# Split output products for the second half of the first span, and a float32 attention product for the second span

## The chip, the cores and the metric

The kernel runs on one core of one Trainium2 chip. The metric is the device time of one execution in microseconds (us), lower is better. The core has a matrix engine (PE) that multiplies a stationary 128x128 operand with a moving one and accumulates in PSUM banks, a vector engine (DVE), a scalar engine (ACT), GpSimd (POOL) and SyncE (SP). In this kernel POOL and SP hardly do more than issue transfers: each has its own queue, and both queues are served by the same 16 DMA engines.

## The reference

Per head: a softmax over the features of q, a softmax over the sequence of k, a 64x64 product k^T v, and q times that product. The heads are joined to rows of 512, and a gated layer follows. All is float32.

```
q_s = exp(q - max(q, axis=-1));  q_s = q_s / (sum(q_s, axis=-1) + 1e-9)
k_s = exp(k - max(k, axis=2));   k_s = k_s / (sum(k_s, axis=2) + 1e-9)
kv  = einsum('bhsd,bhse->bhde', k_s, v)
x   = einsum('bhsd,bhde->bhse', q_s, kv)   # -> (4608, 512)
out = (1 / (1 + exp(-(x @ w_gate))) * (x @ w_val)) @ w_out
```

There are 8 batches of 576 tokens and 8 heads; w_gate and w_val are 512x1536, w_out is 1536x512. The three weights arrive as float64 words.

## The kernel before

The 4608 tokens are worked in nine spans of 512. The first span (span 0) is special: while it runs, the weights are read, narrowed from float64 to float32, split into a high and a low fp32r part, and saved to DRAM for the later spans. It has twelve steps, j = 0 to 11, one for each 128 columns of w_gate and w_val. A step has a first product (`g1_0`, L690: eight float32 matmuls of 512 columns), a sigmoid and a gate product (`g_sig_0` on ACT, `g_mul_0` on DVE, L702), and, one step late, the output product of the step before (`g2_0(j-1)`, L724: four float32 matmuls of 512 columns into the four accumulators). The later spans use three fp32r products of the split parts instead (high x high, high x low, low x high): `g1` (L742, in seven smaller products over sums of blocks) and `g2` (L814), in six steps each.

Beside the first span's matmuls, DVE and ACT narrow the next weights (`w_low`, `w_top`, `w_join`, `wo_...`; L165, L171, L182, L186), cast the parts (`wo_hi` on ACT L244 and `wo_save` on DVE L248, then a POOL transfer; `split_hi` on ACT L293 and `split_lo` on DVE L298, then POOL transfers L303), and prepare the second span: its k, v and q rows (L392, L397, L345), its k^T v (`k_mm`, L420, PE), and its attention product (`x_mm`, L606), which takes three fp32r products per head pair from the parts of q (`qT_hi` on ACT, `qT_lo` on DVE L574) and of k^T v (`kv_hi`, `kv_lo`).

The order on each engine is the order in which the code is written; nothing is reordered. Buffers come from pools, and a semaphore wait stands wherever a buffer is still in use. SP's transfers go through eight semaphores in turn (DMAHW0 to DMAHW7): a transfer waits until the one eight places earlier has landed.

Two places matter further on. One is the end of the first span: step 11 leaves DVE with `split_lo`, the differences `c_lo` (L670) for the next span, `g_mul_0(11)` and the last two `wo_save`. The span's last output product, `g2_0(11)`, stands on PE behind the second span's first `g1`. The other is the third step of the second span: there PE does `k_mm(2)`, which needs rows 0 to 575 of v of batch 2. Rows 0 to 255 lie in two buffers, v_0 and v_1; before, `load_next(1, 5, range(2))` in step 10 asks SP for them, behind the k rows of batch 2.

## Time and profile before

| | us |
|---|---|
| median of 3 runs | 927.94 (927.7 to 928.8) |
| the profiled execution, its own time | 928.79 |
| its span in the profile | 927.0 |
| PE busy | 915.6 (99% of the span) |
| DVE busy | 610.7 (66%) |
| ACT busy | 474.7 (51%) |
| POOL busy | 170.0 (18%) |

The profile gives, for each engine, when its instructions ran and what ended each idle time. "Idle before" with an engine or a DMA behind an arrow says who was waited for. The first span runs from 0 to about 172 us, the second starts its first products at 157 us. Ends of matmuls are modelled, so a group's cost is read from the start of one group to the start of the next.

### The profile page before, as it was taken

How to read it: one execution, taken by the hardware profiler on the slowest of the kernel's cores; microseconds unless marked ns; L12 is line 12 of the kernel's file. 1: busy time of each engine (PE TensorE's matmuls, PEld its weight loads, DVE VectorE, ACT ScalarE, POOL GpSimd, SP SyncE). 2: the span in 40 equal slices, each digit the busy share in tenths (PEclk: the TensorE clock that was granted, in tenths of full speed). 3: DMA queues.
4: the chain of work that ended last, by engine and by line, in shares of the span. 5: the costliest groups of instructions: out<-in, count | busy, mean ns of one | idle time of the engine just before them, and what ended most of it. 6: DMA issues, size and time to landing. Idle time of an engine off the chain costs nothing.

```text
span 927.0 us, 18677 instructions
## 1 busy us (share of the span) xinstructions
PE 915.6 (99%) x7598; PEld 839.6 (91%) x7598; DVE 610.7 (66%) x987; ACT 474.7 (51%) x798; POOL 170.0 (18%) x321
## 2 busy tenths in 40 slices
PE   7999999999999999999999999999999999999998
PEld 7445545899999999999999999999999999999998
DVE  8899979756767577666766667666846574664242
ACT  2777886545445445644563456354725443543222
POOL 0010101312121212212221222112122122212220
PEclk9999999999999999999999999999999999999999
DMA  9987676999999989998999999999997799768761
GB/s 312 371 302 294 256 256 241 396 354 312 260 294 338 321 254 248 337 310 298 240 315 326 292 250 299 317 291 256 303 295 214 226 261 322 235 186 257 213 208 69
DMA packets 93556, 257.97 MB, mean 278 GB/s; under 512 B 15192, under 2 KB 17760, under 8 KB 90528
## 3 DMA queue, kind: packets, MB, share of 16 engines
q0 software_dynamic: 44576, 168.32, 59.8%
q1 hardware_dynamic: 48896, 88.47, 32.2%
q8 instruction: 60, 0.98, 0.5%
q14 instruction: 24, 0.20, 0.1%
HBM read 228.20 MB, written 28.56 MB: 277 GB/s over the span
## 4 chain that ended last, share of the span: by engine, by line
PE 81%; issue 8%; DMA 5%; DVE 4%; POOL 1%; SPq 1%; ACT 0%; POOLq 0%; DVEq 0%
PE gv L742 48%; PE acc L814 28%; DMA wo_raw<-wo_in 2%; PE gv L606 2%; PE at L420 2%; DMA ring<-qf_in 1%; DMA s_sb<-s 1%; DMA lent<-k_in 1%; PE at L606 1%; SPq L385 1%; POOL s L303 1%; DVE f_w L186 0%; POOL wo L251 0%; DVE wo_hl L248 0%; DVE h L702 0%
## 5 line engine op out<-in xcount | busy, mean ns | idle before, releaser
L742 PE MATMUL gv<-c_hl,s_sb 128*128 128x256 f32 x2304 | 277.3, 276 | 0.8 <-DMA s_sb<-s 0.8
L814 PE MATMUL acc<-wo_hl,h 128*128 128x256 f32 x2304 | 269.6, 276 | 0.0
L742 PEld LDWEIGHTS gv<-c_hl,s_sb 128*128 128x128 f32 x2304 | 268.7, 188 | 0.9 <-DVE q_m L498 0.9
L814 PEld LDWEIGHTS acc<-wo_hl,h 128*128 128x128 f32 x2304 | 264.8, 188 | 0.4
L742 PE MATMUL gv<-c_hl,a_w 128*128 128x256 f32 x1728 | 220.8, 277 | 1.9 <-DVE h L702 1.9
L742 PEld LDWEIGHTS gv<-c_hl,a_w 128*128 128x128 f32 x1728 | 207.2, 188 | 3.0 <-DVE h L702 2.1
L310 POOL DMA_DIRECT2D s_sb<-s x188 | 101.4, 539 | 301.5 <-PE gv L742 301.4
L768 DVE TENSOR_TENSOR sg<-gv,sg 128x512 f32<-128x512 f32 x48 | 33.2, 692 | 153.5 <-PE gv L742 153.5
L260 POOL DMA_DIRECT2D wo_hl<-wo x96 | 51.7, 539 | 283.1 <-PE acc L814 280.5
L760 ACT COPY sg<-gv 128x512 f32<-128x512 f32 x48 | 28.2, 588 | 131.8 <-PE gv L742 131.3
L770 ACT COPY sg<-gv 128x512 f32<-128x512 f32 x48 | 28.2, 587 | 104.8 <-PE gv L742 104.8
L772 DVE TENSOR_TENSOR sg<-sg 128x512 f32<-128x512 f32 x48 | 33.2, 692 | 57.3 <-ACT sg L770 57.3
L690 PE MATMUL gv<-x,f_w 128*128 128x512 f32 x160 | 70.2, 593 | 0.0
L690 PEld LDWEIGHTS gv<-x,f_w 128*128 128x128 f32 x160 | 30.0, 190 | 36.3 <-issue 34.5
L793 DVE TENSOR_TENSOR h<-sg,h 128x1024 fp32r<-128x1024 f32 x48 | 58.8, 1226 | 1.6
L781 DVE TENSOR_TENSOR sg<-sg 128x512 f32<-128x512 f32 x48 | 33.2, 693 | 33.6 <-ACT sg L775 33.6
L775 ACT ACTIVATE sg<-sg 128x512 f32<-128x512 f32 x48 | 30.5, 634 | 46.2 <-DVE sg L774 46.2
L762 ACT COPY sg<-gv 128x512 f32<-128x512 f32 x48 | 28.2, 587 | 37.7 <-PE gv L742 37.7
L765 ACT COPY sg<-gv 128x512 f32<-128x512 f32 x48 | 28.2, 587 | 37.2 <-PE gv L742 37.2
L724 PE MATMUL acc<-wo_t,h 128*128 128x512 f32 x96 | 43.2, 592 | 0.0
L724 PEld LDWEIGHTS acc<-wo_t,h 128*128 128x128 f32 x96 | 18.2, 190 | 22.5 <-issue 22.2
L774 DVE TENSOR_TENSOR sg<-gv,sg 128x512 f32<-128x512 f32 x48 | 33.2, 692 | 2.4
(160 smaller groups left out, 999.2 us busy)
## 6 DMA issues: line engine op xcount, KB each, us to landing
s_sb<-s POOLq DMA_DIRECT2D x188, 512.0 KB, 7.3
wo_hl<-wo POOLq DMA_DIRECT2D x96, 512.0 KB, 5.9
s<-s_sb POOLq DMA_DIRECT2D x12, 1024.0 KB, 5.9
out<-x SPq DMA_DIRECT2D x35, 256.0 KB, 5.4
ring<-k_in SPq DMA_DIRECT2D x28, 256.0 KB, 6.0
ring<-qn_in SPq DMA_DIRECT2D x28, 256.0 KB, 4.9
four<-q_m_row SPq DMA_DIRECT2D x56, 128.0 KB, 11.8
ring<-qT_in SPq DMA_DIRECT2D x28, 256.0 KB, 10.3
```

The costliest lines, as they stand in the source:

```text
L260: nc.gpsimd.dma_start(out=t.rearrange("p h e -> p (h e)"), in_=wo_dram[2 * p + i].bitcast(F32R))
L310: nc.gpsimd.dma_start(out=s_sb[:, i].rearrange("p h n e -> p (h n e)"), in_=s_dram[p][:, i * n:(i + 1) * n].bitcast(F32R),)
L690: nc.tensor.matmul(ps[n], lhsT=w[:, kt // 2, sl], rhs=x_0[:, kt], start=(kt == 0), stop=(kt == NK - 1),)
L724: nc.tensor.matmul(acc[0][m], lhsT=h_0[j][:, m * P:(m + 1) * P], rhs=wo_t[j // 2][:, j % 2], start=(j == 0), stop=(j == NJ - 1),)
L742: nc.tensor.matmul(ps[:, n], lhsT=lh(kt), rhs=c_hl[i][:, x, kt], start=(first and n == 0 and kt == 0 and lh is wh and x == 0), stop=(last ...
L768: nc.vector.tensor_tensor(out=sg[:, 0], in0=rr, in1=sg[:, 0], op=ALU.add)
L772: nc.vector.tensor_tensor(out=sg[:, 3], in0=sg[:, 3], in1=sg[:, 2], op=ALU.add)
L774: nc.vector.tensor_tensor(out=sg[:, 1], in0=z, in1=sg[:, 1], op=ALU.add)
L775: nc.scalar.activation(sg[:, 0:2, 0], sg[:, 0:2, 0], AF.Sigmoid)
L781: tt(out=sg[:, 0:2, 0], in0=sg[:, 0:2, 0], in1=sg[:, 0:2, 1], op=ALU.mult)
L793: nc.vector.tensor_tensor(out=lo, in0=sg[:, :, 0], in1=hi.bitcast(F32), op=ALU.subtract)
L814: nc.tensor.matmul(acc[w][m][:, es], lhsT=h[lh][:, i, sl], rhs=o[i][:, rh, es], start=(at == 0 and i == 0 and lh == 0 and rh == 0 and e == 0),
```

## The change

- `g2_0(j)` for j from 6 on is done in three fp32r products with 256 columns each, six matmuls for each accumulator in place of one of 512 float32 columns. The parts of w_out are the ones that `wo_hi` and `wo_save` make for DRAM anyway; they are now kept for the product. The parts of h are new: a cast on ACT (`h_hi_0`) and a subtraction on DVE (`h_lo_0`). `wo_hi(j-1)` and `h_hi_0(j-1)` move to the head of step j on ACT, `wo_save(j-1)` and `h_lo_0(j-1)` stand in front of `w_low` on DVE.
- In step 11 `g_mul_0(11)` moves ahead of the splits on DVE, and so do `wo_save(10)` and `h_lo_0(10)`.
- For steps 10 and 11, h lies in the buffers v_0 and v_1 (v_two). The rows of v of batch 2 that belong there are no longer loaded in step 10, but by `after_second`, behind everything that the second span's first step asks SP for.
- The second span's attention product takes q and k^T v in float32 (`x_mm_1`: two float32 matmuls, of 64 and 448 columns, per head pair). `kv_copy_0` and `kv_copy_1` write the block matrices to v_0 and v_1, `q_copy_1` copies q out of PSUM. `qT_lo`, `qT_hi` and `kv_split(0)` go.
- At the start, operations on neighbouring blocks of q and k are joined (two maxima of 1024 instead of four of 512, and so on), and the last two k blocks get one subtraction and one exponential.
- Of the narrowing, the sign bits of weight tiles 6 and 7 move from DVE to ACT; where DVE still does it, it is one operation on whole words.
- Two k loads and five v loads for the second span stand after step 0 and step 1 instead of in the opening.

On DVE, from the sums of the last split (L272, L273) to the first differences for the next span, before:

```order
L272 TENSOR_TENSOR four_111<-f_last_118 128x512 [waits DVE_49]
L272 TENSOR_TENSOR four_111<-four_111,f_last_118 128x512 [waits DVE_49]
L272 TENSOR_TENSOR four_111<-f_last_118 128x512
L272 TENSOR_TENSOR four_111<-f_last_118,four_111 128x512 [waits DVE_49]
L186 SCALAR_TENSOR_TENSOR wo_t_952<-wo_t_952,wo_raw_903 128x512 [waits Activation_49]
L298 TENSOR_TENSOR a_w_1079<-f_last_118,a_w_1079 128x2x512 [waits Activation_49]
L670 TENSOR_TENSOR c_hl_1061<-x_32_109,c_hl_1061 128x512
```

The same place on DVE now:

```order
L273 TENSOR_TENSOR four_111<-f_last_118 128x512 [waits DVE_49]
L273 TENSOR_TENSOR four_111<-four_111,f_last_118 128x512 [waits DVE_49]
L273 TENSOR_TENSOR four_111<-f_last_118 128x512
L273 TENSOR_TENSOR four_111<-f_last_118,four_111 128x512 [waits DVE_49]
L249 TENSOR_TENSOR wo_hl_1125<-wo_t_962,wo_hl_1125 128x512 [waits DMASW0_49,Activation_49]
L770 TENSOR_TENSOR h_p_1127<-v_0_113,h_p_1127 128x512 [waits Activation_49]
L187 SCALAR_TENSOR_TENSOR wo_t_962<-wo_t_962,wo_raw_896 128x512
L762 TENSOR_TENSOR v_1_114<-gv_1116,v_1_114 128x512 [waits PE_49,Activation_49]
L299 TENSOR_TENSOR a_w_1130<-f_last_118,a_w_1130 128x2x512 [waits Activation_49]
L726 TENSOR_TENSOR c_hl_1107<-x_32_109,c_hl_1107 128x512
```

`wo_save(10)`, the new `h_lo_0(10)` and `g_mul_0(11)` now stand ahead of the splits; before, `wo_save(10)` and `g_mul_0(11)` stood behind the last difference.

On SP, the end of the first span's loads and the second span's first step, before (q_m_row and q_r_row are the maxima and factors of q for the third span, `four` their copies over the partitions, `out` the first span's result, kt the transposed k of batch 3):

```order
L371 DMA ring_1057<-k_in 64x512 [waits DMAHW7_49,DVE_49,Activation_49]
L387 DMA v_0_113<-v_in 128x512 [waits DMAHW0_49]
L387 DMA v_1_114<-v_in 128x512 [waits DMAHW1_49]
L387 DMA f_last_118<-v_in 128x512 [waits DMAHW2_49,PE_49,Activation_49]
L387 DMA f_last_118<-v_in 128x512 [waits DMAHW3_49,PE_49]
L387 DMA f_last_118<-v_in 64x512 [waits DMAHW4_49,PE_49]
L490 DMA q_m_row_1232<-q_m_1227 128x32 [waits DMAHW5_49,DVE_49]
```

SP now, from the transposed k of batch 3 on:

```order
L331 DMA kt_0_115<-kT_in 128x576 [waits DMAHW0_49]
L331 DMA kt_1_116<-kT_in 128x576 [waits DMAHW1_49]
L559 DMA four_111<-q_m_row_1303 64x512 [waits DMAHW3_49,DMAHW2_49]
L559 DMA four_111<-q_m_row_1303 64x512
L559 DMA four_111<-q_m_row_1303 64x512 [waits DMAHW4_49]
L559 DMA four_111<-q_m_row_1303 64x512 [waits DMAHW5_49]
L559 DMA four_111<-q_m_row_1303 64x512 [waits DMAHW6_49]
L559 DMA four_111<-q_m_row_1303 64x512 [waits DMAHW7_49]
L559 DMA four_111<-q_m_row_1303 64x512 [waits DMAHW0_49]
L559 DMA four_111<-q_m_row_1303 64x512 [waits DMAHW1_49]
L398 DMA v_0_113<-v_in 128x512 [waits DMAHW2_49]
L398 DMA v_1_114<-v_in 128x512 [waits DMAHW3_49]
```

The two v loads have moved behind q_m_row, four `out`, two kt and eight `four` transfers, and each of them waits for the landing of a `four` transfer eight places ahead of it (the first and the second).

The diff, cut to its core:

```diff
@@ narrowing
     def narrow_sign_bits(raw):
-        nc.vector.tensor_scalar(
-            out=half(raw, U16, 1), in0=half(raw, U16, 3), scalar1=2 ** 15, scalar2=None,
-            op0=ALU.bitwise_and,
+        low = word(raw, 0)
+        nc.vector.scalar_tensor_tensor(
+            out=low, in0=word(raw, 1), scalar=-2 ** 31, in1=low,
+            op0=ALU.bitwise_and, op1=ALU.bitwise_or,
         )
...
     def w_on_vector(j):
-        return j in (1, 6, 7)
+        return j == 1
@@ second span's attention product
+    kv_1 = [v_two[b].rearrange("p (h e) -> p h e", e=P) for b in range(2)]
...
+    def x_mm_1(hp):
+        x_ps[1, hp] = ps = ps_at.tile([P, T], F32, name="at")
+        q = q_1.pop(hp)
+        for b, f, t in x_parts(1):
+            nc.tensor.matmul(
+                ps[:, f:t], lhsT=kv_1[b][:, hp], rhs=q[:, f:t],
+                start=True, stop=True, skip_group_check=True,
+            )
@@ output product of the first span
     def g_sig_0(j):
-        h_0[j] = two.tile([P, T], F32, name="h_0", tag="h_lo")
+        if j < J3:
+            h_0[j] = two.tile([P, T], F32, name="h_0", tag="h_lo")
+        else:
+            h_0[j] = v_two[j % 2] if j > 9 else ring.tile([P, T], F32, name="ring")
...
+    def h_hi_0(j):
+        h_hl[0, j] = t = two.tile([P, 2, T], F32R, name="h_p", tag="h_lo")
+        nc.scalar.copy(out=t[:, 0], in_=h_0[j])
+
+    def h_lo_0(j):
+        t = h_hl[0, j]
+        nc.vector.tensor_tensor(
+            out=t[:, 1], in0=h_0.pop(j), in1=t[:, 0].bitcast(F32), op=ALU.subtract
+        )
...
+            h, o = h_hl[0, j], wo_out[j]
+            for lh, rh in ((0, 0), (0, 1), (1, 0)):
+                for e in range(2):
+                    es = slice(e * HT, (e + 1) * HT)
+                    nc.tensor.matmul(
+                        acc[0][m][:, es], lhsT=h[:, lh, sl], rhs=o[:, rh, es],
...
@@ loads
         if j == 10:
             k_max_rows(2)
-            load_next(1, 5, range(2))
+            load_next(1, 5, ())
...
+    def after_second():
+        for t in range(2):
+            v_load(2, t)
@@ start
     k_exp(0, 0)
-    for c in range(NC):
-        qn_sub(0, c)
-        qn_exp(0, c)
+    for c in (0, 2):
+        qn_sub(0, c, 2)
+        qn_exp(0, c, 2)
...
-    for t in ORDER_0[1:]:
+    for t in (3, 4):
         k_sub(0, t)
         k_exp(0, t)
         k_mm_0(t, kv0)
-    for c in range(NC):
-        qn_sum(0, c)
+    k_subs(0, 1, 3)
+    k_exps(0, 1, 3)
+    k_mm_0(1, kv0)
+    k_mm_0(2, kv0)
+    qn_sum(0, 0, NC)
     warm(12)
@@ steps of the first span
         beside_first(j)
+        if j > 0:
+            wo_hi(j - 1)
+        if j > J3:
+            h_hi_0(j - 1)
...
         wo_join(j)
+        if j > J3:
+            wo_save(j - 1)
+            h_lo_0(j - 1)
...
@@ step 11
     g1_0(j)
+    wo_hi(j - 1)
+    h_hi_0(j - 1)
+    g_sig_0(j)
     split_hi(p, (0, 3))
-    wo_hi(j - 1)
+    wo_save(j - 1)
+    h_lo_0(j - 1)
     wo_join(j)
-    g_sig_0(j)
+    g_mul_0(j)
     g2_0(j - 1)
@@ later spans
                 side_b(w + 1, at)
+            if (w, at) == (1, 0):
+                after_second()
```

## Rows read from the trace of the kernel before

**Rows 1.** The page's first part (busy time and share of each engine), and the waits of PE after its first matmuls, from the view of who waited for whom (total us, times, longest).

```profile
PE 915.6 (99%) x7598; PEld 839.6 (91%) x7598; DVE 610.7 (66%) x987; ACT 474.7 (51%) x798; POOL 170.0 (18%) x321
...
PE gv L742 <- DVE h L702: 1.9, 1, 1.9
```

**Rows 2.** PE in order of time: start, duration, what. Steps 9 to 11 of the first span (counted from 0), then the second span up to its fourth step.

```profile
132.52 3.60 PE L724 MATMUL acc<-wo_t,h 128*128 128x512 f32 x8
...
136.90 7.03 PE L690 MATMUL gv<-x,f_last 128*128 128x512 f32 x16
143.77 3.60 PE L724 MATMUL acc<-wo_t,h 128*128 128x512 f32 x8
147.20 0.27 PE L355 MATMUL at<-ident,k_max 128*4 128x128 f32 x1
...
169.29 3.59 PE L724 MATMUL acc<-wo_t,h 128*128 128x512 f32 x8
...
175.06 3.06 PE L742 MATMUL gv<-c_hl,s_sb 128*128 128x256 f32 x24 [0.76 <-DMA s_sb<-s]
...
199.25 1.15 PE L420 MATMUL at<-v,ring 128*64 128x64 f32 x32
...
201.87 5.72 PE L814 MATMUL acc<-wo_hl,h 128*128 128x256 f32 x48
207.43 1.52 PE L742 MATMUL gv<-c_hl,a_w 128*128 128x256 f32 x12
```

**Rows 3.** All engines in order of time, the opening: PE's k^T v product (L405), its filler matmuls (L1042), ACT's exponentials of k (L397), the transposes of q (L552).

```profile
16.85 2.35 ACT L397 ACTIVATE lent<-lent 128x512 f32<-128x512 f32 x4
17.57 2.38 PE L405 MATMUL acc<-lent 128*64 128x65 f32 x64
...
19.88 2.94 PE L1042 MATMUL gv<-lent 128*128 128x128 f32 x24
22.66 0.60 PE L552 MATMUL gv<-ident,lent 128*128 128x128 f32 x4
```

**Rows 4.** DVE in order of time, from the gate product of step 9 to the third span's first maxima.

```profile
132.72 0.69 DVE L702 TENSOR_TENSOR h<-gv,h 128x512 f32<-128x512 f32 x1 [1.61 <-PE gv L690]
...
155.38 0.69 DVE L670 TENSOR_TENSOR c_hl<-x,c_hl 128x512 fp32r<-128x512 f32 x1
156.50 1.23 DVE L298 TENSOR_TENSOR s_sb<-four,s_sb 128x1024 fp32r<-128x1024 f32 x1 [0.43 <-ACT s_sb L293]
...
163.59 1.28 DVE L248 TENSOR_TENSOR wo_hl<-wo_t,wo_hl 128x512 fp32r<-128x512 f32 x2
...
172.79 2.46 DVE L498 TENSOR_REDUCE q_m<-ring 128x8 f32<-128x512 f32 x4
```

**Rows 5.** SP's issues in order of time (start, time until the last of the group was issued, what).

```profile
159.52 2.88 SPq L387 DMA_DIRECT2D v<-v_in  x2
...
175.28 0.34 SPq L490 DMA_DIRECT2D q_m_row<-q_m  x1
175.71 1.81 SPq L717 DMA_DIRECT2D out<-x  x4
177.56 0.99 SPq L329 DMA_DIRECT2D kt<-kT_in  x2
181.85 12.98 SPq L530 DMA_DIRECT2D four<-q_m_row  x8
195.74 0.33 SPq L490 DMA_DIRECT2D q_r_row<-q_r  x1
197.31 1.66 SPq L537 DMA_DIRECT2D ring<-qT_in  x2
```

**Rows 6.** DMA issues of short stretches (KB of each, median us from issue to landing): the v rows at 159.4 to 161.3 us, the first `four` at 178 to 182, those at 182 to 184, and the first q^T row at 197 to 198.5; then DVE's work on those q^T rows by the view of the tile `four`.

```profile
v<-v_in SPq DMA_DIRECT2D x1, 256.0 KB, 6.5
...
four<-q_m_row SPq DMA_DIRECT2D x1, 128.0 KB, 13.8
...
four<-q_m_row SPq DMA_DIRECT2D x3, 128.0 KB, 14.9
...
ring<-qT_in SPq DMA_DIRECT2D x1, 256.0 KB, 11.2
...
L541 DVE TENSOR_TENSOR ring<-ring,four x4: 684/692/694, 208.6 to 211.6; 128x512 f32<-128x512 f32 x4
```

**Rows 7.** Stretches: busy time of PE, PEld, DVE, ACT and POOL (instructions), granted PE clock, DMA share, GB/s. The last two are of the very start.

```profile
195.00:200.00 5.00, 5.00 (x62) 4.87 (x62) 2.74 (x5) 3.08 (x5) 1.08 (x2) 1.00 1.32 300
200.00:205.00 5.00, 5.00 (x89) 4.87 (x86) 2.62 (x5) 0.00 (x0) 0.00 (x0) 1.00 1.37 340
...
3.00:4.00 1.00, 1.00 (x6) 1.00 (x6) 0.96 (x2) 0.00 (x0) 0.00 (x0) 1.00 1.04 340
...
10.00:11.00 1.00, 1.00 (x12) 1.00 (x11) 1.00 (x2) 0.00 (x0) 0.00 (x0) 1.00 1.03 383
```

**Rows 8.** PE at the very start, in order of time: the filler matmuls, the transposes of k behind the first pause, the next fillers.

```profile
1.14 5.84 PE L1042 MATMUL gv<-lent 128*128 128x128 f32 x32 [1.14 <-POOL lent L1005]
9.38 0.63 PE L1056 MATMUL acc<-ident,lent 128*128 128x128 f32 x4 [2.40 <-DVE lent L1053]
9.85 1.50 PE L1042 MATMUL gv<-lent 128*128 128x128 f32 x12
```

**Rows 9.** POOL in order of time: the first load of the sums' weights (s_sb) for the second span's second step; it stands right behind the save of the last w_out tile.

```profile
165.91 0.54 POOL L310 DMA_DIRECT2D s_sb<-s  x1
```

More of the change, by code (lines that the diff above doesn't have):

```diff
@@ L36 @@
 ORDER_0 = (0, 3, 4, 1, 2)
+J3 = 6
 NF = 2
@@ L340, in k_max, with k_max_1 @@
             out=kneg[b][:, hp:hp + 1], in0=m, scalar1=-1.0, scalar2=None, op0=ALU.mult
+        )
+    def k_max_1():
+        kmax[1], kneg[1], ksum[1] = (
+            small.tile([P, NP], F32, name=f"k_{x}") for x in ("max", "neg", "sum")
+        )
+        nc.vector.tensor_reduce(out=kmax[1].unsqueeze(2), in_=k1T, axis=AX.X, op=ALU.max)
+        nc.vector.tensor_scalar(
+            out=kneg[1], in0=kmax[1], scalar1=-1.0, scalar2=None, op0=ALU.mult
         )
@@ L392, in k_sub, with k_subs @@
         eng.tensor_tensor(out=kt[:n], in0=kt[:n], in1=kmb[b][:n], op=ALU.subtract)
+    def k_subs(b, t0, t1):
+        kt = k_rows[b][:, t0:t1]
+        m = kmb[b].unsqueeze(1).broadcast_to([P, t1 - t0, DM])
+        nc.vector.tensor_tensor(out=kt, in0=kt, in1=m, op=ALU.subtract)
     def k_exp(b, t):
@@ L475, in attn_moe, with qn_of @@
     qn_sb = {}
+    q_rows = {}
+    def qn_of(w, c, n):
+        if n == 1:
+            return qn_sb[w, c]
+        return q_rows[w][:, c:c + n].rearrange("p c (i d) -> p (c i) d", d=D)
     q_m = {}
@@ L515, in qn_sum @@
         nc.vector.tensor_reduce(
-            out=q_r[w][:, c * TI:(c + 1) * TI], in_=t, axis=AX.X, op=ALU.add
+            out=q_r[w][:, c * TI:(c + n) * TI], in_=t, axis=AX.X, op=ALU.add
         )
-        if c == NC - 1:
+        if c + n == NC:
             t = q_r[w]
@@ L610, in x_mm, with kv_copy_0, kv_copy_1, q_copy_1 @@
                     )
+    q_1 = {}
+    kv_1 = [v_two[b].rearrange("p (h e) -> p h e", e=P) for b in range(2)]
+    def kv_copy_0():
+        for b in range(2):
+            nc.scalar.copy(out=kv_1[b], in_=kv_0)
+    def kv_copy_1():
+        for a in range(2):
+            sl = slice(a * D, (a + 1) * D)
+            nc.scalar.copy(out=kv_1[1][sl, :, sl], in_=kv_32[1](sl))
+    def q_copy_1(hp):
+        q_1[hp] = t = ring.tile([P, T], F32, name="ring")
+        nc.scalar.copy(out=t, in_=qT_sb.pop((1, hp)))
+    def x_mm_1(hp):
[5 more added lines that the diff above has]
+                start=True, stop=True, skip_group_check=True,
+            )
     def x_ev(w, hp):
@@ L723, in g2_0 @@
         for m in range(NT):
-            nc.tensor.matmul(
-                acc[0][m], lhsT=h_0[j][:, m * P:(m + 1) * P], rhs=wo_t[j // 2][:, j % 2],
-                start=(j == 0), stop=(j == NJ - 1),
-            )
+            sl = slice(m * P, (m + 1) * P)
+            if j < J3:
+                nc.tensor.matmul(
+                    acc[0][m], lhsT=h_0[j][:, sl], rhs=wo_t[j // 2][:, j % 2],
+                    start=(j == 0), stop=False, skip_group_check=True,
+                )
+                continue
+            h, o = h_hl[0, j], wo_out[j]
+            for lh, rh in ((0, 0), (0, 1), (1, 0)):
+                for e in range(2):
+                    es = slice(e * HT, (e + 1) * HT)
+                    nc.tensor.matmul(
+                        acc[0][m][:, es], lhsT=h[:, lh, sl], rhs=o[:, rh, es],
+                        start=False, stop=(j == NJ - 1 and lh == 1 and e == 1),
+                        skip_group_check=True,
+                    )
         if j == NJ - 1:
@@ L941, in behind_joins @@
             kv_lo(1)
-        if 6 <= j <= 9:
-            qT_lo(1, j - 6)
     def after_first(j):
         if j == 0:
-            for hp in range(NP):
-                k_max(1, hp)
+            k_max_1()
+            for t in range(3, 5):
+                k_load(1, t)
         if j == 1:
@@ L952, in after_first @@
                 qn_max(1, c)
+            for t in range(5):
+                v_load(1, t, v1[t])
         if j == 2:
@@ L1031, in attn_moe @@
         qn_load(1, c)
-    for t in range(5):
+    for t in range(3):
         k_load(1, t)
-    for t in range(5):
-        v_load(1, t, v1[t])
+    q_rows[0] = q0
+    k_rows[0] = k0
     idle = ps_gv.tile([P, T], F32, name="gv")
@@ L1087, in attn_moe @@
         k_mm_0(t, kv0)
-    for c in range(NC):
-        qn_sum(0, c)
+    k_subs(0, 1, 3)
[3 more added lines that the diff above has]
+    qn_sum(0, 0, NC)
     warm(12)
-    for hp in range(NP):
-        qf_mul(0, hp)
-        if hp == 0:
-            k_done_0(kv0)
+    qf_mul(0, 0)
+    k_done_0(kv0)
+    qf_mul(0, 1, NC - 1)
     w_low(0)
@@ L1194, in attn_moe @@
     wo_hi(j)
-    g_mul_0(j)
-    wo_save(j - 1)
+    h_hi_0(j)
     wo_save(j)
+    h_lo_0(j)
     def wo_next(w, at):
```

61 lines of the change are left out of this document (32 added, 29 removed).

## The prediction

> **What bounds the kernel now.** I read the page's first part, the waits of PE, PE in order of time, then the same stretch on DVE, on SP's queue and by landings. PE is busy 99% of the span [rows 1]. From its first weight product on, each group starts where the one before ends, but for two waits: 1.9 us for a DVE result at the end of the first span [rows 1] and 0.76 us for a weight load [rows 2]. So each us saved on PE counts, as long as nothing that PE waits for is late. The reader is to see two things that already run close. DVE works through the first span's end without a pause but for 0.43 us [rows 4]. And from about 160 us on both DMA queues are full: in the third step of the second span they move 300 to 340 GB/s with a DMA share of 1.3 [rows 7], and what SP asks for takes 11 to 15 us to land [rows 6].
>
> **The opening.** PE does the last two k blocks from 19.2 us on and starts 12 fillers (24 instructions) at 19.88; the transposes of q follow at 22.66 without a pause, so the opening ends on PE [rows 3]. Now the last two exponentials are one, behind a subtraction that is one too; I reckon its end at about 19.3 instead of 16.85 + 2.35 = 19.2. Only then PE starts two blocks, not one. Four blocks took 2.31 us (17.57 to 19.88), 0.58 each, so the fillers start at about 20.5, and all behind them is 0.6 us later. The bounds are 0, if the joined operations on DVE bring the exponential forward by as much, and 0.8. What they save shortens a chain that doesn't end here, so I take +0.6.
>
> **The output products.** Float32 costs 143.77 to 147.20, 3.43 us a step. Three fp32r products in the later spans take 201.87 to 207.43, 5.56 for 48, so 2.78 for 24 [rows 2]. Six steps save 0.65 each, 3.9 us. The bound below is 0: if the kept parts come late, PE waits instead.
>
> **The attention product.** Step 9 takes 4.38 us from its output product to the next first product; less 3.43 this leaves 0.95 for six fp32r matmuls [rows 2]. Float32 with 448 columns is 448/512 of 0.858, 0.75; the 64 columns cost between 0.11 (in proportion) and 0.23, a filler of 128 columns (24 instructions in 2.78, two to a matmul [rows 3]). So 0.86 to 0.98: I take no change, four times. DVE loses `qT_lo`, four times 0.6 us, and ACT gets `kv_copy` in its place; both lie beside step 6's first product of 6.9 us.
>
> **The casts.** `h_lo_0` costs DVE 0.6 us each (two of this form in 1.28 [rows 4]). PE waits for it at the fifth of six matmuls, about 0.45 us into the group. At the end that bites: from the gate product of step 9, which waits for PE, DVE has 32.15 us of work until `wo_save(11)` is through (132.72 to 164.87 [rows 4]); now 1.2 more, less the pause of 0.43. With the opening's +0.6 and two cheaper products, PE ends step 9's first product at 132.0 instead of 132.52; so DVE ends at 165.0 instead of 164.87. PE gets no faster than that: `c_lo(B11)`, at 155.38 before [rows 4], now has `wo_save(10)`, `h_lo_0(9)`, `h_lo_0(10)` and `g_mul_0(11)` ahead of it, starts at 157.2, and the second span's first products follow DVE. They end about 167.7 instead of 169.29. The wait of 1.9 us is gone, since the gate product that it was for is early; waits for the casts, by the same reckoning some 0.3, 1.1 and 1.2 us in steps 8, 10 and 11, take its place. `g2_0(11)` is 0.65 cheaper: the second step starts 2.2 us earlier. Its load of s_sb is issued at 165.7 as before (165.91, landed 174.92 [rows 2, 9]), since it stands behind `wo_save(11)`; between 6.5 and 9 us of landing PE is 2.6 to 0.3 us ahead there. Half a MB of v and half a MB of w_out no longer stand right before it, some 2.5 us at 400 GB/s, so I take the upper end. **If nothing else moved**, PE would reach `k_mm(2)` at 196.6 instead of 199.25, and the time would be 927.94 - 2.6 = 925.3.
>
> **The v rows.** Here the change pays. `k_mm(2)` begins with v_0 and v_1. Before, they were asked for at 159.52 [rows 5] and had 40 us. Now they stand behind q_m_row, `out`, kt and eight `four`, and each waits for the landing of one of the first two `four`. Before, those were issued from 181.85 on and landed after 13.8 and 14.9 us, at 195.65 and 197.2; the two transfers that stood in that place, q_r_row and the first q^T row, were issued at 195.74 and 197.31 to the landing [rows 5, 6]. What sets this chain is `q_m_row`, which follows DVE's maxima after the second span's first step; I have that 1.5 us earlier. So v_0 goes out at about 194, v_1 at 195.5. PE wants them at 196.6 and 197.1. Bounds of the landing: a 256 KB row of v took 6.5 us at 160 us [rows 6], which gives v_1 at 201.5 to 202. The first q^T row took 11.2, landed at 208.5, and DVE started on it at 208.6 [rows 6]: the same size, the same place behind the `four`. With 1.5 us less and one more row that is v_1 at 207.7. I take 205.7, near the upper end, since POOL's queue, which shares the engines, has its last requests 2.6 us earlier and half a MB less. PE's first matmul on v_1 was at 199.25 + 0.49. The time moves by 205.7 - 199.7 = **+6.0 us**, between +1.8 and +8.0, whatever PE won before: all gains ahead of this wait become wait. Behind PE's wait stand `g2` of the second span and all that follows, in the order of the code; the q^T rows, which now land behind v, are due 6 us later too.
>
> Of the queues: SP's transfers got about 87 GB/s while POOL's were queued (128 KB every 1.5 us). The Trainium skill's page "DMA: Bandwidth & Descriptors", section "Queues, rings and completion order", says that each DMA engine goes round in turn between the queues that have work; the trace agrees, and by it SP speeds up once POOL's queue is empty.
>
> **The clock.** PE would stand idle some 9 us. The trace has one pause to compare: 2.40 us, after which 12 fillers' instructions come at full pace [rows 8]. The other end is the start, after doing nothing: 6 matmuls in a us where later 12 fit, 32 in 5.84 us [rows 7, 8] where 24 took 2.78 [rows 3], so 2.1 us lost, though the clock column says 1.00 throughout [rows 7]. 6 a us against 12 are the two levels, 1.2 and 2.4 GHz. Bounds 0 and 2.1; I take 2.1, since nine us of nothing are nearer to a start than to 2.4 us.
>
> The Trainium skill's page "TensorE: Matmul & The Clock Gate", Part 1, says that an idle engine falls back to half its clock and must work to regain it. By it the whole 2.1 us is due; by the one pause of the trace alone, none.
>
> **The sum.** Profiled execution: 928.79 + 6.0 + 2.1 = 936.9, its span 927.0 + 8.1 = 935.1. It lies 0.85 above the median, so from 927.94: **936.0**.
>
> **The rivals.** (a) The wait comes, the clock holds: +6.0, 933.9. For it: the pause of 2.40 us cost nothing. (b) The v rows land at the quick end, 201.5 to 203.5: +1.8 to +3.8, about 930.7. For it: 6.5 us once; against it: eight `four` ahead in a full queue. (c) The other side: v lands before PE wants it, and the gain of 2.6 us stays, 925.3. It decides at the landing of v_1: faster if that is before 199.7 minus 1.9, that is within 2.3 us of its issue, or if SP reaches these rows much earlier than the chain q_m_row, `out`, kt, `four` lets it. The rows give no such landing. (d) In between, v_1 at 198 to 201.5: within 1.9 us of before. (e) The split products aren't cheaper than float32: PE comes to `k_mm(2)` at 199 or later and waits there just the same; the time is that of the forecast, and only PE's rows would tell.
>
> **Chances.** Forecast with the clock lost 0.50; (a) 0.17; (b) 0.15; (d) 0.10; (c) 0.08; (e) is inside the first two. A measurement of this kernel can tell about 0.2%, 1.9 us, from no change. So slower 0.82, same 0.10, faster 0.08. The range leaves out (c) and most of (d): from 929.7, the quick landing without clock loss, to 939.0, which is +8.0 and 2.1 with 0.9 on top for the opening and for what I took too early on SP.
>
> **What would show it.** Right: one wait of PE of 7 to 11 us in the second span, at the first or second group of `k_mm(2)`, ended by a v row; v_0 issued at 193 to 195 us; matmuls behind it at half the pace for a few us. Right on the small steps: first weight product at 29.4 to 29.6 instead of 28.87; output products of 2.7 to 2.8 us; no wait for the gate product at the end of the first span. Wrong, if v lands before PE comes, if the wait is below 3 us, or if PE stalls for something else, above all for the casts of steps 9 and 10 by more than 2 us.

## The result, and the profile after

The changed kernel takes **940.42 us** (median of 4 runs, 938.1 to 941.04) beside 928.37 us for the kernel before (4 runs, 927.7 to 931.07): ratio 1.0115, 95% interval 1.0096 to 1.0135. The profiled execution of the changed kernel is 940.6 us long with a span of 938.6, so 11.6 us of span more than before. All executions on record are undisturbed ones; the ratios with their intervals are estimates over them and not the quotients of the two medians beside them.

The waits of PE (us in total, times, longest), from the view of who waited for whom, changed kernel. Waits of its first 30 us are left out:

```profile
PE at L440 <- DMA v<-v_in: 6.7, 2, 5.9
PE gv L824 <- DMA s_sb<-s: 2.7, 1, 2.7
...
PE acc L805 <- DVE wo_hl L249: 1.1, 2, 0.7
...
PE gv L824 <- DVE c_hl L726: 0.3, 1, 0.3
```

The wait for the gate product at the end of the first span [rows 1] is gone. Four others are there, and the first is the one forecast: PE waits for the rows of v. PE in order of time (start, duration, what), changed kernel; L747 is the first product of a step, L805 the output product in three parts, L663 the attention product, L583 the transposes of q, L824 a product of the later spans' steps, L440 the k^T v product, L894 the later spans' output product:

```profile
29.10 1.45 PE L747 MATMUL gv<-x,f_w 128*128 128x512 f32 x3
...
120.40 3.43 PE L805 MATMUL acc<-wo_hl,h_p 128*128 128x256 f32 x24
123.67 1.14 PE L663 MATMUL at<-ring,v 128*128 128x64 f32 x4
124.64 0.60 PE L583 MATMUL gv<-ident,ring 128*128 128x128 f32 x4
...
143.58 3.22 PE L805 MATMUL acc<-wo_hl,h_p 128*128 128x256 f32 x22 [0.65 <-DVE wo_hl L249]
...
167.91 2.88 PE L805 MATMUL acc<-wo_hl,h_p 128*128 128x256 f32 x24
170.63 1.52 PE L824 MATMUL gv<-c_hl,a_w 128*128 128x256 f32 x12
174.85 4.58 PE L824 MATMUL gv<-c_hl,s_sb 128*128 128x256 f32 x24 [2.70 <-DMA s_sb<-s]
...
198.31 1.52 PE L824 MATMUL gv<-c_hl,a_w 128*128 128x256 f32 x12
205.78 1.12 PE L440 MATMUL at<-v,ring 128*64 128x64 f32 x16 [5.95 <-DMA v<-v_in]
207.65 1.12 PE L440 MATMUL at<-v,ring 128*64 128x64 f32 x16 [0.74 <-DMA v<-v_in]
208.56 2.97 PE L440 MATMUL at<-f_last,ring 128*64 128x64 f32 x48
211.46 7.89 PE L894 MATMUL acc<-wo_hl,h 128*128 128x256 f32 x48
219.19 1.52 PE L824 MATMUL gv<-c_hl,a_w 128*128 128x256 f32 x12
```

Set beside [rows 2] this gives the whole loss. The fourth step of the second span begins at 219.19 instead of 207.43, 11.76 later, and from there to the end both kernels need the same (927.0 - 207.43 = 719.6; 938.6 - 219.19 = 719.4). The 11.76 have two parts. The first matmul on the second v row stands at 207.65; before, it came 0.49 behind 199.25. That is **7.9 us** of lateness. From there to the fourth step the changed kernel takes 11.54 us and the kernel before 7.69, for the same instructions: **3.85 us**. The output product of this stretch shows it best: 7.89 us instead of 5.72.

Why it is slow there is in the stretches (busy time of PE, PEld, DVE, ACT and POOL, then the granted PE clock, DMA share, GB/s), changed kernel, to be held beside [rows 7]:

```profile
170.00:175.00 5.00, 2.30 (x20) 2.13 (x20) 4.97 (x9) 4.04 (x9) 3.02 (x6) 1.00 1.10 397
175.00:180.00 5.00, 5.00 (x31) 5.00 (x32) 2.47 (x5) 1.11 (x2) 1.24 (x3) 0.66 1.13 369
...
200.00:205.00 5.00, 0.00 (x0) 0.00 (x0) 3.19 (x5) 0.45 (x2) 0.00 (x0) 0.74 1.15 372
205.00:210.00 5.00, 3.48 (x60) 3.29 (x62) 1.68 (x3) 0.00 (x0) 0.00 (x0) 0.50 0.76 277
210.00:215.00 5.00, 5.00 (x42) 4.76 (x39) 3.19 (x9) 0.00 (x0) 0.00 (x0) 0.50 0.62 183
215.00:220.00 5.00, 5.00 (x42) 5.00 (x41) 0.00 (x0) 0.00 (x0) 0.78 (x2) 0.89 0.96 298
```

The granted clock falls to 0.50, the lower level of 1.2 GHz, while PE does nothing, and stays there for all of 205 to 215 (in stretches of 1 us: 1.00 until 202, 0.50 from 203 to 216, 1.00 from 217 on). A second, shorter fall, to 0.66 on average, stands at 175 to 180, behind the wait of 2.70 us for `s_sb`: the 24 matmuls there take 4.58 us instead of 2.88.

SP's issues in order of time, changed kernel, beside [rows 5]:

```profile
173.89 0.34 SPq L517 DMA_DIRECT2D q_m_row<-q_m  x1
...
180.05 14.16 SPq L559 DMA_DIRECT2D four<-q_m_row  x8
195.07 2.21 SPq L398 DMA_DIRECT2D v<-v_in  x2
197.94 0.33 SPq L517 DMA_DIRECT2D q_r_row<-q_r  x1
```

And the time from issue to landing (KB each, median us), from the DMA issues of 180 to 184 and of 195 to 196.9, changed kernel, beside [rows 6]:

```profile
four<-q_m_row SPq DMA_DIRECT2D x4, 128.0 KB, 15.2
...
v<-v_in SPq DMA_DIRECT2D x1, 256.0 KB, 10.7
```

The v rows stand where the queue's order puts them, behind the copies `four`: asked for at 195.07, landed 10.7 us later, at 205.8, when PE's wait ends. Before, they were asked for at 159.52.

POOL in order of time, changed kernel, beside [rows 9]; L304 stores parts of the last sums' weights, L311 loads those of the next step:

```profile
159.48 0.53 POOL L304 DMA_DIRECT2D s<-s_sb  x1 [1.01 <-DVE s_sb L299]
...
168.39 0.55 POOL L311 DMA_DIRECT2D s_sb<-s  x1 [2.42 <-PE gv L824]
```

The load was issued at 168.39 instead of 165.91, yet it landed at 174.7, about where it did before (174.9). The page names PE as what ended the idle time, but that product ended at 162.5. What the load overwrites is read by the store of 159.48, which took 8.3 us to land; that fits, 167.8. In the kernel before, the same store was issued at 158.13 and took 6.8 us. It was issued 1.35 later because DVE's cast for it stands at 157.86 instead of 156.50 [rows 4]: the casts and the gate product moved ahead of the splits push it back.

### The profile page after: what moved, and what is told of

Read it like the earlier page. It is cut to its first block, busy times and chain, and to the rows that moved or that the text cites. A ratio compares the mean times of both kernels' runs of the same rounds, so it can differ in the third digit from the quotient of the medians.

```text
span 938.6 us, 18849 instructions
## 1 busy us (share of the span) xinstructions
PE 918.4 (98%) x7686; PEld 850.8 (91%) x7686; DVE 608.3 (65%) x969; ACT 483.3 (51%) x805; POOL 171.5 (18%) x321
## 4 chain that ended last, share of the span: by engine, by line
PE 83%; issue 6%; DMA 5%; DVE 4%; ACT 1%; POOL 1%; SPq 0%; POOLq 0%; DVEq 0%; ACTq 0%
PE gv L824 46%; PE acc L894 28%; PE gv L747 3%; PE at L440 2%; PE gv L637 2%; DMA four<-q_m_row 2%; DMA v<-v_in 1%; PE acc L796 1%; DMA q_m_row<-q_m 1%; PE at L637 1%; DMA lent<-k_in 1%; POOL wo L252 0%; DMA s<-s_sb 0%; DVE c_hl L726 0%; PE acc L686 0%
## 5 line engine op out<-in xcount | busy, mean ns | idle before, releaser
L824 PE MATMUL gv<-c_hl,s_sb 128*128 128x256 f32 x2304 | 278.7, 277 | 2.8 <-DMA s_sb<-s 2.7
L824 PEld LDWEIGHTS gv<-c_hl,s_sb 128*128 128x128 f32 x2304 | 270.0, 189 | 3.1 <-DVE ring L532 2.9
L894 PE MATMUL acc<-wo_hl,h 128*128 128x256 f32 x2304 | 271.6, 278 | 0.0
L894 PEld LDWEIGHTS acc<-wo_hl,h 128*128 128x128 f32 x2304 | 266.8, 189 | 0.5
L824 PE MATMUL gv<-c_hl,a_w 128*128 128x256 f32 x1728 | 219.8, 276 | 0.3 <-DVE c_hl L726 0.3
L824 PEld LDWEIGHTS gv<-c_hl,a_w 128*128 128x128 f32 x1728 | 206.8, 188 | 0.5 <-DVE c_hl L726 0.5
L311 POOL DMA_DIRECT2D s_sb<-s x188 | 102.2, 544 | 303.2 <-PE gv L824 300.7
L747 PE MATMUL gv<-x,f_w 128*128 128x512 f32 x160 | 70.2, 593 | 0.0
L747 PEld LDWEIGHTS gv<-x,f_w 128*128 128x128 f32 x160 | 30.0, 190 | 36.3 <-issue 35.0
L872 DVE CAST h<-sg 128x1024 fp32r<-128x1024 f32 x48 | 33.2, 693 | 1.4
L570 DVE TENSOR_TENSOR ring<-ring,four 128x512 f32<-128x512 f32 x28 | 18.6, 690 | 20.9 <-DMA ring<-qT_in 19.0
```

The source lines that it names most:

```text
L311: nc.gpsimd.dma_start(out=s_sb[:, i].rearrange("p h n e -> p (h n e)"), in_=s_dram[p][:, i * n:(i + 1) * n].bitcast(F32R),)
L747: nc.tensor.matmul(ps[n], lhsT=w[:, kt // 2, sl], rhs=x_0[:, kt], start=(kt == 0), stop=(kt == NK - 1),)
L824: nc.tensor.matmul(ps[:, n], lhsT=lh(kt), rhs=c_hl[i][:, x, kt], start=(first and n == 0 and kt == 0 and lh is wh and x == 0), stop=(last ...
L872: nc.vector.tensor_copy(out=hi, in_=sg[:, :, 0])
L894: nc.tensor.matmul(acc[w][m][:, es], lhsT=h[lh][:, i, sl], rhs=o[i][:, rh, es], start=(at == 0 and i == 0 and lh == 0 and rh == 0 and e == 0),
```

## The experiments

Theory A: the time is lost at one place, since the v rows have lost their place in SP's queue; PE's idle time then costs clock. Its rivals: the loss comes from the split products and their casts; the half clock has nothing to do with PE's pause. The later runs ask where the gain that PE had made by then went.

**The v rows moved, nothing else.** The kernel before, with the two loads put behind the copies:

```diff
-            load_next(1, 5, range(2))
+            load_next(1, 5, ())
...
+            if (w, at) == (1, 0):
+                for t in range(2):
+                    v_load(2, t)
```

> The kernel before, with one part of the change alone: rows 0 to 255 of v of batch 2 are asked for behind the second span's first step. Theory A (their place in SP's queue is the loss): the chain q_m_row, out, kt, four stands where it stood, 1.4 us later than in the changed kernel, so v_1 lands at about 209 us, PE waits 8 to 10 us at k_mm(2) and loses some 4 us more at half clock: 939 to 942 us. Rival B (the casts and split products of the first span are the loss): this run is like the kernel before, 927.5 to 930 us.

Measured: 940.6 us, ratio 1.0123 (1.0099 to 1.0146): all of the change's loss, without any of its products. PE in order of time, this kernel:

```profile
207.57 1.98 PE L420 MATMUL at<-v,ring 128*64 128x64 f32 x32 [9.70 <-DMA v<-v_in]
...
217.37 1.52 PE L742 MATMUL gv<-c_hl,a_w 128*128 128x256 f32 x12
```

PE came at 197.9 and waited 9.70 us: v_0, asked for at 196.91, landed 1.8 us later than in the changed kernel, where it was asked for at 195.07. From the landing to the fourth step it takes 9.80 us where the kernel before takes 8.18 from the same matmul: 1.6 us of half clock here.

**The change with the v rows ahead of the copies.**

```diff
+            if (w, at) == (1, 0):
+                after_second()
             if not last:
                 side_b(w + 1, at)
-            if (w, at) == (1, 0):
-                after_second()
```

> The changed kernel, with the two v loads asked for behind out, ahead of kt and the eight four transfers. Theory A: v goes out at about 177 us, lands in 8 to 14 us, by 191, and PE, which comes at 199.8, does not wait: the 7.9 us of wait and the 3.9 us behind it go, 928 to 930 us. Rival B: as slow as the changed kernel, 938 us or more. Rival C (the DMA queues are so full there that the place does not matter): v lands after 200 us, 931 to 938.

Measured: 930.78 us beside 928.93, ratio 1.0025 (1.0008 to 1.0042). The rows are asked for at 176.5 and PE doesn't wait for them. So the loss of 12 us is the place in the queue: moving the rows alone brings all of it, and moving them back takes nearly all of it away. What remains, some 0.2%, is at another place, as the rows of PE show, this kernel:

```profile
175.20 4.57 PE L824 MATMUL gv<-c_hl,s_sb 128*128 128x256 f32 x24 [2.80 <-DMA s_sb<-s]
...
200.90 1.15 PE L440 MATMUL at<-v,ring 128*64 128x64 f32 x32
```

PE waits for `s_sb`, runs partly at half clock behind it (0.66 in 175 to 180), and so comes to the k^T v product 1.65 us later than before.

**The clock.** The changed kernel with 24 float32 filler matmuls ahead of the k^T v product, into columns of its PSUM tile that nothing reads.

```diff
...
+            if b == 2:
+                for _ in range(24):
+                    nc.tensor.matmul(
+                        at[:, T - P:T], lhsT=ident, rhs=ident, start=True, stop=True,
+                        skip_group_check=True,
+                    )
```

> The changed kernel, with 24 float32 matmuls of 128 columns ahead of k_mm(2) on PE, about 5.6 us of work that no result needs, in the time in which PE waits for v. Theory A's second half (the 3.9 us behind the wait are the clock's): granted clock 1.00 from 205 to 220 us, the wait for v is the same, k_mm and the product behind it run at full pace: 936 to 937.5 us. Rival D (they are slow for the transfers that land beside them): 940 us as before, at a clock of 1.00.

Measured: 938.5 us, ratio 1.0095 (1.0073 to 1.0117); span 935.1 instead of 938.6. PE in order of time, this kernel:

```profile
199.24 5.52 PE L440 MATMUL at<-ident 128*128 128x128 f32 x48
206.04 0.69 PE L447 MATMUL at<-v,ring 128*64 128x64 f32 x16 [1.28 <-DMA v<-v_in]
207.92 0.69 PE L447 MATMUL at<-v,ring 128*64 128x64 f32 x16 [1.19 <-DMA v<-v_in]
...
215.62 1.52 PE L831 MATMUL gv<-c_hl,a_w 128*128 128x256 f32 x12
```

and two of its stretches, the clock again in the third column from the end:

```profile
205.00:210.00 5.00, 2.77 (x80) 2.56 (x80) 1.27 (x3) 0.00 (x0) 0.00 (x0) 1.00 0.85 305
210.00:215.00 5.00, 5.00 (x49) 4.93 (x46) 3.55 (x10) 0.00 (x0) 0.54 (x1) 1.00 0.49 166
```

The v rows land as late as in the changed kernel. With PE kept busy the granted clock is 1.00 in every stretch from 200 to 220, and 207.92 to 215.62 is 7.70 us, what the kernel before needs. So in the profiled executions the whole 3.85 us was the clock, and PE's pause was its cause; slow matmuls at a clock of 1.00, the rival, did not come. The times show less of it: the profiled execution, 937.0, is the fastest of the four, the median lies above the 936 to 937.5 that I expected, and the ratio's interval overlaps that of the changed kernel.

**The v rows behind the last cast**, where the first span has done with the two buffers that they land in (in the changed kernel these hold h of its last two steps):

```diff
+    after_second()
+
     def wo_next(w, at):
...
-            if (w, at) == (1, 0):
-                after_second()
```

> The changed kernel, with the two v loads asked for right behind the last cast of the first span, ahead of q_m_row. Theory A: no wait at k_mm(2). The 512 KB now stand beside the load of s_sb that PE waits 2.7 us for: by 400 GB/s that wait grows by up to 1.3 us. 928.5 to 931.5 us, 0 to 1.5 above the run with v behind out. Rival B: 938 or more.

Measured: 930.54 us, ratio 1.0016 (1.0004 to 1.0027). Again no wait for v; the wait for `s_sb` is 3.40 us, the granted clock behind it 0.50 in 175 to 180.

**All output products in float32, v late** (`J3 = 12`, no casts of h, and the last w_out parts saved behind the products as before the change):

```diff
-J3 = 6
+J3 = 12
...
```

> The changed kernel with all twelve output products of the first span in float32 and no casts of h, the w_out parts saved behind the products as in the kernel before; opening, attention products and the late v rows stay. Theory A (all that PE wins ahead of the v rows becomes wait): the v rows land where they did, within a us, since q_m_row follows DVE; PE comes 1 to 4 us later and waits 2 to 5 us instead of 6; 939.5 to 941.5, the same as the changed kernel. Rival E (the split products carry their saving to the end): 3.9 more, 944.3.

Measured: 941.46 us (938.33 to 943.84), ratio 1.0145 (1.013 to 1.016). That is somewhat above the changed kernel's 1.0115, with intervals that touch, so the times alone don't decide between A and E; the rows do. PE in order of time, this kernel:

```profile
205.22 1.12 PE L440 MATMUL at<-v,ring 128*64 128x64 f32 x16 [7.89 <-DMA v<-v_in]
207.16 1.12 PE L440 MATMUL at<-v,ring 128*64 128x64 f32 x16 [0.81 <-DMA v<-v_in]
```

The v rows land 0.5 us earlier and PE waits 8.7 us for them, so the products' price is taken up by that wait and can't reach the end. One thing came out against what I wrote: PE comes to the v rows not later than in the changed kernel but earlier, at 197.3 against 199.8, although six products cost more. It waits only 0.84 us for `s_sb` at 173.6 and loses no clock there. By then the change's split products, with their casts, had won nothing, and the next runs ask why.

**The rest of the loss: fillers at the wait for `s_sb`.** The kernel with v ahead of the copies, and fillers into the product's own tile ahead of its first matmul:

```diff
+        if (w, p) == (1, 0):
+            for _ in range(12):
+                nc.tensor.matmul(
+                    z[:, 0, 0:P], lhsT=ident, rhs=ident, start=True, stop=True,
+                    skip_group_check=True,
+                )
         prod(z, wsum(S1), T1, True, False)
...
```

> The v rows ahead of the copies (b), and on PE 12 float32 fillers of 128 columns (24 instructions, 2.8 us) ahead of the S1 product of the second span's second step, where b waits 2.80 us for s_sb and then runs 24 matmuls in 4.4 us at a granted clock of 0.66 instead of in 2.8. The fillers write to the product's own PSUM tile ahead of its first matmul and add nothing to the result. Theory S (what is left of the loss in b is this wait and the half clock behind it): the 24 matmuls take 2.8 us again, the clock column shows 1.00 in 175 to 180, the load lands when it did, so the time is 1.6 lower than b's 930.8: 929.2. Rival T (the slow matmuls have another cause, the loads beside them for instance): still 4.4 us, 930.8 or more.

Measured: 931.53 us, ratio 1.0019 (1.0005 to 1.0033). PE in order of time, this kernel:

```profile
174.71 3.00 PE L824 MATMUL gv<-c_hl,s_sb 128*128 128x256 f32 x24
...
206.21 1.52 PE L824 MATMUL gv<-c_hl,a_w 128*128 128x256 f32 x12
...
226.62 2.93 PE L824 MATMUL gv<-c_hl,s_sb 128*128 128x256 f32 x12 [2.57 <-ACT sg L842]
```

Half of what I expected came. The clock stays at 1.00 in 175 to 180 and the 24 matmuls take 3.00 instead of 4.57: theory S holds there, and the fourth step starts at 206.21, 1.2 ahead of the kernel before. But the time does not follow. DVE multiplies the q^T rows as they land behind the copies, here until 214.8, in the kernel before until 212.3; ACT's exponentials come behind that, and PE waits 2.57 us for ACT in the fifth step, with half clock behind it. A gain of 1.2 us had met the next transfer. Four of the twelve executions took 928.1 to 928.7 us; whether this second wait is missing in them no profile shows.

**The store that the load waits for.** Two ways to let it land earlier, both with v ahead of the copies: the 512 KB store of a w_out tile behind the sums' stores; and step 10's product back in float32, by which that w_out store moves behind the sums' stores too.

```diff
...
     wo_hi(j)
     h_hi_0(j)
+    wo_store(j - 1)
     wo_save(j)
...
```

> b, with the store of the eleventh w_out tile's parts (512 KB) issued on POOL behind the two stores of the last sums' parts, right ahead of the store of the twelfth, instead of ahead of them. The load of s_sb S1 overwrites what the first of these two stores reads, and was issued 8.8 us after it in b (159.73 to 168.54) and 7.8 us in the kernel before (158.13 to 165.91). Theory S (the 512 KB ahead slow that store): it lands in 7.5 us instead of 8.4, the load is issued at about 167.3, PE waits 1.6 instead of 2.8 us; 929.5 if the clock still falls, 927.9 if it does not. Rival U (the delay is DVE's order, the store's place does not matter): load at 168.2 to 168.6 and 930.8.

```diff
-            if j < J3:
+            if j < J3 or j == 10:
...
-    wo_hi(j - 1)
-    h_hi_0(j - 1)
     g_sig_0(j)
     split_hi(p, (0, 3))
-    wo_save(j - 1)
-    h_lo_0(j - 1)
     wo_join(j)
...
+    wo_hi(j - 1)
     wo_hi(j)
     h_hi_0(j)
+    wo_save(j - 1)
     wo_save(j)
...
```

> b, with the output product of the eleventh step of the first span in float32 as in the kernel before, and its w_out parts saved with the twelfth's. DVE loses 0.6 us, and another 0.6 moves behind the sums; the 512 KB store moves behind the sums' stores too. Theory S: first store of the last sums at 158.5, landed 7.5 us later, load of S1 issued at 166.0 to 166.3, PE (0.65 more in this product, 0.5 less of waits for casts) comes at 172.3 and waits 0.7 to 1.5 us; no half clock behind it; 928.0 to 928.8, level with the kernel before or better. Rival U (the load is late for another reason, landing at 175 whatever its issue): 930.8.

Measured: 929.92 us, ratio 1.0011 (0.9999 to 1.0023), and 929.52 us, ratio 1.0006 (0.9996 to 1.0016), beside 929.02. In the first the load is issued at 167.88, 0.7 earlier than in the run with only the rows moved ahead (168.54), lands at 175.2, and PE still waits 2.87 us. In the second, PE in order of time:

```profile
169.68 1.52 PE L824 MATMUL gv<-c_hl,a_w 128*128 128x256 f32 x12
174.83 4.59 PE L824 MATMUL gv<-c_hl,s_sb 128*128 128x256 f32 x24 [3.62 <-DMA s_sb<-s]
```

The load is issued at 165.89, as before the change, takes 8.8 us and still lands at 174.7. That is what the rival said of the landing, 175 whatever the issue; the time, 929.5, fits neither theory's forecast. PE came earlier and waited longer. Both kernels are within measurement of the kernel before.

**Less ahead of the load.** If the bytes queued ahead set the landing, the two w_out stores (1 MB) have to go behind it. Three runs: the stores behind the load of S1, with v behind the last cast and with v ahead of the copies, and, for comparison, 14 fillers with v behind the last cast and the stores where they were.

```diff
...
         more(S1)
+        if (w, p) == (1, NS - 1):
+            wo_store(10)
+            wo_store(11)
...
```

> The v rows asked for behind the last cast (d), and the stores of the eleventh and twelfth w_out tiles' parts (512 KB each, on POOL ahead of the load of s_sb S1 until now) issued right behind that load. Where the load was issued 2.6 us earlier (step 10's product in float32) it landed at 174.8 all the same, in 8.9 us. Theory Q (the load's landing is set by what the DMA engines still have to move ahead of it): 1 MB less ahead is some 2.6 us at 400 GB/s, it lands at 172.0 to 173.0 instead of 175.4, PE waits under 1 us instead of 3.4, its clock stays at 1.00 and the 24 matmuls take 2.8 instead of 5.3: 4 to 5 us less than d's 930.5, less what then waits for the copies of the fifth step; 926.5 to 928.5. Rival U (landing follows something else, the last sums' store for instance): 174.5 to 175.5 and 930.5.

> b (v rows right ahead of the copies) with the same two stores behind the load of S1. Theory Q: lands at 171.5 to 172.5, PE waits for under 0.5 us, clock 1.00; ahead of the fifth step that is 4 us less than b. Theory V (the copies of the fifth step, which stand behind the v rows on SP here, take it again): the wait for ACT comes back as in e, 2 to 3 us with half clock behind it; so 929 to 931, and i is the faster one by 1.5 or more. Without V: 926.5.

> d and 14 float32 fillers of 128 columns (28 instructions, 3.25 us) on PE ahead of the same product, written to its own PSUM tile ahead of its first matmul. Theory S (the half clock behind the wait is PE's pause): 1.00 in 175 to 185, 24 matmuls in 2.8 instead of 5.3 and 12 in 1.36 instead of 1.64: 2.7 less than d, 927.8, as long as the copies of the fifth step land in time; in e the v rows stood ahead of these copies and DVE was through with the q^T rows at 214.8, here I expect 210.8 as in d and no wait there. Rival V (the copies take the gain again): PE waits for ACT in the fifth step, 930 or more.

Measured: 933.65 us, ratio 1.0043 (1.0031 to 1.0056); 931.57 us, ratio 1.0027 (1.0011 to 1.0043); 929.88 us, ratio 1.0008 (0.9997 to 1.002), beside 928.9. PE in order of time, the first of them (v behind the casts):

```profile
174.12 1.62 PE L829 MATMUL gv<-c_hl,s_sb 128*128 128x256 f32 x12 [1.56 <-DVE q_m L530]
177.87 2.90 PE L829 MATMUL gv<-c_hl,s_sb 128*128 128x256 f32 x12 [2.13 <-DMA s_sb<-s]
```

Not as expected: slower, not faster. S1's half comes 1.3 earlier than without the move, and S2's, whose load now stands behind the stores, is 2.13 us late instead. With v ahead of the copies S2's wait is the same, and PE's wait for ACT in the fifth step is back (2.5 us), as expected for it; but that this run would be 1.5 or more slower than the first was wrong, it is 2.1 faster. In it the clock stayed at 1.00 behind the wait of 2.14 us; in the first it fell to 0.50 behind the 2.13, and the twelve matmuls took 1.3 more. The fillers do what they should: clock 1.00 throughout, S1's product at 175.75, k^T v at 200.27. PE doesn't wait for ACT here. Its k^T v product is still 1.0 behind [rows 2], since PE can go no faster than that landing, and so the time stays above the 927.8 that I expected.

**The stores behind all four loads**, with v behind the casts and 8 fillers:

```diff
...
         more(S4)
+        if (w, p) == (1, NS - 1):
+            wo_store(10)
+            wo_store(11)
...
```

> The v rows behind the last cast (d), the same two w_out stores behind all four loads of the next sums instead of between the first and the second of them, and 8 float32 fillers (16 instructions, 1.9 us) ahead of the S1 product. In the run with the stores between the loads the wait split: S1's product began at 174.1 and S2's at 176.4 to 177.9. Theory Q (each landing follows the bytes queued ahead of it): with none of the two stores ahead, S1 lands at 173.5 to 174.5 and S2 within 1.5 us of it, PE's waits there sum to under 1 us, clock 1.00, the w_out loads still come before 185; the second step is 1.3 ahead of the run with 14 fillers: 928.0 to 929.0. Rival U (landing at 175 whatever is ahead): waits of 1.5 us or more, and 930 or more.

Measured: 937.41 us, ratio 1.0089 (1.0073 to 1.0105), where I expected 928 to 929. PE in order of time, this kernel:

```profile
174.23 2.98 PE L829 MATMUL gv<-c_hl,s_sb 128*128 128x256 f32 x24
...
186.31 8.42 PE L908 MATMUL acc<-wo_hl,h 128*128 128x256 f32 x48 [3.65 <-DMA wo_hl<-wo]
...
198.41 4.58 PE L829 MATMUL gv<-c_hl,s_sb 128*128 128x256 f32 x24 [2.26 <-DMA s_sb<-s]
```

The sums' wait is gone: the load, issued at 166.04, landed 7.1 us later, at 173.1, where I had expected 173.5 to 174.5. That the two stores ahead set the landing is not shown by it: in the float32 run both stood ahead of the load, issued at 165.81, and it landed at 173.4. And the w_out parts are stored at 172.83 instead of 165.3 and read back from 179.73 on instead of 172.47. They come 3.65 us late, POOL's next loads stand behind them and come 2.26 late, and both waits cost clock. None of these kernels beats the kernel before; the nearest are level with it.

## Why the prediction was right and where it was wrong

**Right: direction, place and mechanism.** The v rows' place in SP's queue is the loss (moved alone: 1.0123; put back: 1.0025 and 1.0016), the wait is one of v at the first and second group of `k_mm(2)`, and the gains ahead of it become wait (float32 throughout: PE comes 2.5 us earlier and waits until about the same time). The wait is shorter than the 7 to 11 us forecast, 5.95 and 0.74, since PE came later than I thought. Rivals (a) to (d) did not come: v was neither quick nor in time, and the clock did not hold. Rival (e) came in its sign: PE reached `k_mm(2)` at 199.8, later than in the kernel before. The split products did get cheaper, by 0.16 to 0.7 us each, but the gain was lost on the way, as said below.

**Wrong by size: the clock.** The term was 2.1 us, and 2.1 was also its upper bound; it measured 3.85. The step that failed took the price of a lost clock from the kernel's start, as if that were the most it could cost. PE ran at 0.50 from 205.8 to 216 here, so longer than the start's 5.84 us. In two other runs behind waits of 9.7 and 8.7 us the same loss was 1.6 and 2.0 us (207.16 to 216.81 is 9.65 us in the float32 run, against 7.69). The start's price lies in the middle of these. It was an instance, not a bound. The Trainium skill's page "TensorE: Matmul & The Clock Gate", Part 1, says that an idle engine falls to half its clock; the trace agrees, with 0.50 in these stretches and 1.00 once fillers kept PE busy.

**Wrong by size: v.** 6.0 us was forecast within +1.8 and +8.0; it measured 7.9. My upper landing for v_1, 207.7, was right to 0.1 us, but by two errors that cancel: it went out at 196.95 instead of 195.5 and took 10.7 us. The copies were issued 1.8 earlier (1.5 forecast), but the first took 15.0 us to land instead of 13.8, so v_0 went out at 195.07 instead of about 194. The step that failed is the 2 us that I shaved off the upper landing because POOL's last requests would be 2.6 us earlier. They were not: POOL's load of S3 was issued at 197.52 and that of S4 at 198.88 (196.90 and 198.31 before), since POOL follows PE there, and PE had no lead. And the reason itself does not hold: in the float32 run these loads were issued at 195.03 and 196.38, v_0 went out 1.0 earlier, and v_1 still landed only 0.5 earlier. The two sizes together are 3.65 us, the distance from the 936.9 forecast for the profiled execution to its 940.6.

**What stood behind the missing lead: the issue of a load.** I let PE be 2.6 us ahead from the load of `s_sb` on, with the load issued at 165.7 as before and landing in 6.5 us. The landing took 6.3 us, but the load goes out at 168.39. I had it stand behind `wo_save(11)` alone and left out that it waits for the sums' store, which the casts on DVE made late; in six runs with that store the load went out 0.6 to 0.7 us behind its landing. An earlier issue would not have brought the lead either: with the split products the load landed at 174.4 to 175.7 in the seven other runs, issued anywhere from 165.9 to 168.5, unless the two w_out stores were put behind it (172.9 to 174.0). Why is only in part known; the kernel before with the v rows moved, in which both stores stand right ahead of the load, has it issued at 166.26 and landed at 173.6. So PE waited 2.70 us there, lost 1.7 more to the half clock, got some 0.7 back because its products from 179 to 199 ran a little faster than before (5.44 us instead of 5.65 for an output product; why stays open), and came to `k_mm(2)` at 199.8 instead of 196.6. In the changed kernel it cost nothing, being hidden by v. It is what is left in the kernels in which v comes in time: there "if nothing else moved", 925.3, would have been wrong by some 4.5 us.

**The small steps.** The opening cost 0.23 us, not 0.6 (first weight product at 29.10). The output products were the term most off among them: the eighth step's takes 120.40 to 123.67, 3.27 us, where I had 2.78, so it saves 0.16 and not 0.65. The weight load of its fifth matmul waits 0.28 us for `h_lo_0`, which ends at 121.16, by the rows of PEld; PE's own list has no such wait. Only the last one, for which the casts are long through, takes 2.72 (167.91 to 170.63). The attention product is 0.97, as said. PE's listed waits are 0.65 and 0.45 for the casts in steps 10 and 11 and 0.26 for a difference behind them, where I had 0.3, 1.1 and 1.2 in steps 8, 10 and 11. DVE is through with `wo_save(11)` at 165.0, as forecast, and the second span's first products end at 167.91 (forecast 167.7).

What stays open: when the clock comes back. It was 0.50 from 203 to 216 us in the changed kernel, from 201 to 211 in the run with v alone and from 202 to 211 in the float32 run, although the waits end between 205.2 and 207.6 in all three. So the loss goes with how much work falls ahead of the return and not with the length of the wait, and nothing here shows what sets the return. It varies between executions of one kernel too, as far as the mean granted clock tells: 0.994 in the changed kernel's execution of 938.1 us, 0.991 in those of 940.6 and 941.04. Open is also why, with all products in float32, the load of `s_sb` issued at 165.81 landed at 173.4, and with five split products, issued at 165.89, at 174.7.

## What to carry to other kernels

A load that moves in program order moves in a queue: look at what stands ahead of it there and when that lands, before counting what the compute saves. Where two gates follow each other closely (here the sums' load at 175, the v rows, the copies for the fifth step), a gain ahead of a gate is worth only the distance to it, and moving bytes from ahead of one gate puts them ahead of the next. An instance of a price (a pause, a clock loss) seen once in a trace is no upper bound; widen it. If PE must wait anyway, fillers that are shorter than the wait keep its clock, as they did here; whether time is won by it depends on the next gate.
